# The first block's softmax sums on GpSimd's queue, with SyncE modelled in the kernel's plan

## The chip, the cores and the metric

The kernel runs on one core of a Trainium2 chip. A core has five engines that run side by side, each with its own order of instructions: TensorE (PE in the profile, with PEld for its weight loads) multiplies matrices, VectorE (DVE) and ScalarE (ACT) work element by element, GpSimd (POOL) does small work on the side, and SyncE (SP) issues DMAs. An engine that waits for a semaphore holds up everything behind it in its own order; a queue of DMAs is such an order too. The metric is the device time of one execution in microseconds (us), the median of several runs.

## What is computed

One transformer block: attention with 32 heads of 20 columns over 2048 rows, then a gated bilinear layer. The reference, cut to what matters (the feature size is 640, the gated layer's width 1728, all in bf16):

```python
qkv = (x @ wqkv).reshape(B, S, 3, H, Dh).transpose(2, 0, 3, 1, 4)
scores = einsum("bhqd,bhkd->bhqk", q, k) * (Dh ** -0.5)
o = einsum("bhqk,bhkd->bhqd", softmax(scores), v)
return o.transpose(0, 2, 1, 3).reshape(B, S, D) @ wo      # A

h  = x + A(layernorm(x), wqkv, wo)
ln = layernorm(h)
out = h + ((ln @ w_gate) * (ln @ w_up)) @ w_down
```

## The kernel before

**Tiles.** The 32 heads form eight groups of four (numbered 0 to 7), each head in a slot of 32 partitions. The queries are cut into four blocks of 512. Scores are computed transposed, keys on the partitions, into "score tiles" of 1536 columns (`sc`, two buffers in PSUM). ScalarE turns each into exponentials (`E`, line 612). VectorE can take the last 512 columns of a score tile from it and compute the exponentials there by a polynomial (lines 648 to 659); ScalarE then does only 1024. TensorE multiplies the exponentials with the values (line 836) into `acc`; a column of ones beside the values makes that product carry the sum of the exponentials too.

**Order of the work.** The first query block (b = 0) of groups 0 to 3 goes through the keys in four chunks of 512 rows, since keys and values are made on the way: chunk by chunk, rows are loaded, normalized on VectorE (`gen_ln`, with a power on GpSimd), transposed into `lnT`, and projected. The second chunk's four row tiles (t = 4 to 7) are transposed on TensorE (`on_pe`, `job_T`), the later chunks' by SP's transposing DMA (`turn`, `T_of`). Groups 4 to 7 follow over all keys at once, and their projections are made while earlier groups run. After b = 0 the other blocks follow, and each finished block's output projection and gated layer (the "tail") is worked in between the exponentials of the next.

**The plan.** One Python loop emits score tile after score tile and keeps clocks of its own (`at["pe"]`, `at["dve"]`, `at["exp"]` for ScalarE, in ns) to decide what goes in between. Three kinds of work fill the room:

- *jobs* for TensorE (projections, transposes, tails) stand in a queue and are Python generators that yield the ns of a piece; a job that yields `WAIT` is set aside in `waiting`, and `step` tries the next job, unless that one has the same key but for its kind. `ensure` forces a job whose result the next score tile needs.
- *aux* work for VectorE (normalizing, products) is stepped by `spare` when the plan's VectorE clock has room. `ensure_aux` forces it.
- *events*, registered by `later(n, fn)`, run n score tiles on.

**K and Q projections** (`job_pair`): ten matmuls into the bank `mi`, an evacuation to one of five staging tiles `st` by VectorE (line 275), then a transposing DMA on SP into `kT` or `qa`/`qb` (line 349). `read_at` tells the plan when the result can be read: 2.4 us (`MOVE_NS`) after the evacuation. Value projections (`job_vp`) need no DMA.

**Dividing by the sums** (`norm`, lines 697 to 736): each finished group's product `asb` holds four rows of sums (one per head). They are written to DRAM (line 704), read back spread over all partitions (line 705), inverted on VectorE (`back`, line 715), written to DRAM again (line 717), and read as four broadcasts (`spread`, line 722); then `times` multiplies (line 726). All seven DMAs stand on SP's queue. The second DMA of each pair is issued `TRIP` = 2 score tiles after the first. `back` comes five tiles after the copy of `asb`, and not before 6 us (`SUMS_NS`) on the plan's clock; the multiplication eight tiles after that. This is done for 42 pieces, eight of them of the first block; the rest of the groups (`FAST`) go by TensorE.

**The output weights** (`load_wo`): eight tiles, each cleared by VectorE (line 1024) and filled by four DMAs on SP (line 1031). It is an aux generator, queued behind the projections of groups 4 to 7.

## Time and profile before

| | us |
|---|---|
| median of 3 runs | 911.85 (911.7 to 914.49) |
| the profiled execution | 911.6 |
| its span, first to last instruction | 909.8 |
| ScalarE busy in it | 854.0 |
| VectorE busy in it | 752.5 |
| mean granted TensorE clock | 0.98 |

The page gives each engine's busy time and its share of the span. A view of windows gives the same by stage: engine by engine the busy us of a stretch, with the number of instructions in brackets, then the granted clock of TensorE, the share of the DMA engines in use and the GB/s moved. A row of the timeline is: start and length in us, engine, line of the kernel, operation, what it writes and reads, how many were merged (x2), and in square brackets how long the engine stood idle before it and what ended the wait. A row of the grouped view gives shapes and count, then busy us and the mean ns of one, then the idle us before. SPq is SP's queue of DMA issues: the length there is the issue, not the transfer.

### The profile page before, as it was taken

To read this page: it belongs to the slowest core of one execution; us is meant where nothing else is said; L and a number is where in the kernel's file an instruction comes from. 1 tells how busy PE (TensorE), PEld (TensorE's weight loads), DVE (VectorE), ACT (ScalarE), POOL (GpSimd) and SP (SyncE) were. 2 spreads that over 40 slices of the span, in tenths; PEclk is the share of its full clock that TensorE was granted. 3 is DMA by queue.
4 is the path that set the end of the run, shared out by engine and by line. 5 is a ranking of instruction groups with operands and counts; after the bars stand their busy time and mean duration, and the time that the engine had idled before them with its cause. 6 is when DMAs were issued, how large, how long until landed. Compare 5 with 4: busy or idle time off the path is not lost.

```text
span 909.8 us, 23209 instructions
## 1 busy us (share of the span) xinstructions
PE 814.8 (90%) x9452; PEld 408.6 (45%) x9452; DVE 752.5 (83%) x1431; ACT 854.0 (94%) x719; POOL 31.7 (3%) x163
## 2 busy tenths in 40 slices
PE   8879998979989889989988999998889989889997
PEld 6434554534223334544434445444434444435475
DVE  7678888968989989897998998998998998964242
ACT  6889999979999999999999999999999999999941
POOL 3100000000001100001000000000001000010000
PEclk9879999989999999999999999999999999999999
DMA  6342224344024455432205324302453112011310
GB/s 196 59 76 36 43 52 72 65 77 78 14 68 124 119 140 179 137 83 52 64 9 151 91 59 124 87 16 57 121 132 95 50 27 66 10 29 43 80 45 19
DMA packets 146722, 69.26 MB, mean 76 GB/s; under 512 B 73288, under 2 KB 143604, under 8 KB 146608
## 3 DMA queue, kind: packets, MB, share of 16 engines
q1 hardware_dynamic: 146608, 67.70, 30.4%
q8 instruction: 76, 1.25, 0.6%
q14 instruction: 38, 0.31, 0.1%
HBM read 48.91 MB, written 7.28 MB: 62 GB/s over the span
## 4 chain that ended last, share of the span: by engine, by line
ACT 58%; PE 19%; issue 15%; DVE 6%; DMA 2%; SPq 1%; ACTq 0%; DVEq 0%
ACT E L612 46%; ACT El L612 12%; PE sc L595 4%; PE acc L836 3%; PE mi L345 3%; PE mi L1207 2%; PE f L1189 2%; PE f L1256 1%; PE mi L545 1%; DMA xs<-in_A_x_dram 1%; DVE st L275 1%; DVE xe L653 1%; DMA sums_all<-sums 1%; PE mi L366 1%; DVE xt L659 0%
## 5 line engine op out<-in xcount | busy, mean ns | idle before, releaser
L612 ACT ACTIVATE E<-sc 128x1536 bf16<-128x1536 f32 (+1 forms) x559 | 701.7, 1403 | 14.1 <-PE sc L595 13.9
L595 PE MATMUL sc<-qa,kT 32*128 32x256 bf16 (+1 forms) x2176 | 206.2, 323 | 22.8 <-ACT E L612 15.3
L595 PEld LDWEIGHTS <-kT 32*128 32x128 bf16 x3136 | 85.8, 92 | 209.2 <-issue 168.6
L648 DVE TENSOR_SCALAR xv<-sc 128x512 f32<-128x512 f32 x198 | 136.4, 689 | 42.6 <-PE sc L595 38.4
L836 PE MATMUL acc<-E,vx 128*32 128x256 bf16 (+1 forms) x2268 | 158.5, 319 | 0.5 <-ACT E L612 0.5
L612 ACT ACTIVATE El<-sc 128x1536 bf16<-128x1536 f32 (+1 forms) x124 | 156.4, 1344 | 1.2 <-PE sc L595 1.0
L653 DVE SCALAR_TENSOR_TENSOR xe<-xt,xv 128x512 int16<-128x512 f32 x198 | 133.5, 681 | 0.7
L659 DVE SCALAR_TENSOR_TENSOR xt<-xt,xv 128x512 f32<-128x512 f32 x198 | 133.1, 680 | 0.7
L658 DVE SCALAR_TENSOR_TENSOR xt<-xv 128x512 f32<-128x512 uint16 x198 | 132.4, 682 | 0.3
L836 PEld LDWEIGHTS <-vx 128*32 128x32 bf16 x3136 | 62.3, 96 | 59.7 <-issue 57.8
L595 PE MATMUL sc<-qb,kT 32*128 32x256 bf16 (+1 forms) x960 | 68.4, 279 | 8.1 <-ACT E L612 5.1
L345 PE MATMUL mi<-wqk,lnT 128*128 128x160 bf16 x600 | 59.0, 242 | 14.7 <-DVE st L275 8.4
L1207 PE MATMUL mi<-ln2T,wu 128*128 128x256 bf16 x410 | 60.2, 277 | 7.7 <-DVE hh L1215 7.3
L1207 PE MATMUL mi<-ln2T,wg 128*128 128x256 bf16 x410 | 58.7, 274 | 8.2 <-DVE u L1212 8.2
L545 PE MATMUL mi<-kT,ident 128*128 128x512 bf16 x192 | 57.9, 383 | 5.2 <-DVE xr L1260 2.2
L345 PEld LDWEIGHTS <-lnT 128*128 128x128 bf16 x600 | 44.5, 101 | 39.4 <-issue 39.1
L1256 PE MATMUL mi<-wd,hh 128*128 128x320 bf16 x350 | 60.5, 301 | 0.9 <-DVE xr L1260 0.8
L836 PE MATMUL acc<-xe,vx 128*32 128x256 bf16 (+1 forms) x305 | 57.2, 310 | 0.0
L836 PE MATMUL acc<-El,vx 128*32 128x256 bf16 (+1 forms) x563 | 54.4, 295 | 0.0
L1256 PEld LDWEIGHTS <-hh 128*128 128x128 bf16 x448 | 38.0, 98 | 28.2 <-issue 16.6
L1207 PEld LDWEIGHTS <-wu 128*128 128x128 bf16 x410 | 35.3, 98 | 30.4 <-issue 25.4
L1207 PEld LDWEIGHTS <-wg 128*128 128x128 bf16 x410 | 35.7, 97 | 29.4 <-issue 26.0
(143 smaller groups left out, 621.6 us busy)
## 6 DMA issues: line engine op xcount, KB each, us to landing
wu<-in_B_w_up_dram SPq DMA_DIRECT2D x38, 320.0 KB
wg<-in_B_w_gate_dram SPq DMA_DIRECT2D x38, 320.0 KB
bc<-scr SPq DMA_DIRECT2D x60, 64.0 KB
bc<-scr SPq DMA_DIRECT2D x108, 32.0 KB
qsp<-qa SPq DMA_DIRECT2D x8, 384.0 KB
xr<-in_A_x_dram SPq DMA_DIRECT2D x16, 160.0 KB
out_dram<-xr SPq DMA_DIRECT2D x14, 160.0 KB
wd<-in_B_w_down_dram SPq DMA_DIRECT2D x13, 160.0 KB
```

What stands on the lines that cost most here:

```text
L345: nc.tensor.matmul(ps[:, k * PAIR:(k + 1) * PAIR], lhsT=lnT[:, c, (2 * tt + k) * P:(2 * tt + k + 1) * P], rhs=wqk[gp // 2][c][:, m, lo:lo ...
L545: nc.tensor.matmul(ps[:], lhsT=ident[:], rhs=kT[0][:, 0:2].rearrange("p t g k -> p (t g k)"), start=True, stop=True)
L595: nc.tensor.matmul(by_tile(sc[:, o:o + w]), lhsT=kT[g // 2][SLOT * j:SLOT * (j + 1), kt, g % 2, :], rhs=q_of(g, b, c0, w)[SLOT * j:SLOT * ...
L612: exps = nc.scalar.activation(e[:, 0:n_act], sc[:, 0:n_act], ACT.Exp, bias=EXP_BIAS, scale=SM_SCALE)
L648: took = nc.vector.tensor_scalar(v[:], ps, X_SCALE, X_BASE, ALU.mult, ALU.max)
L653: nc.vector.scalar_tensor_tensor(e[:], t[:], X_R, v[:], ALU.mult, ALU.add)
L658: lambda: nc.vector.scalar_tensor_tensor(t[:], u, X_P, u, ALU.add, ALU.mult),
L659: lambda: nc.vector.scalar_tensor_tensor(t[:], t[:], X_Q, u, ALU.add, ALU.mult),
L836: nc.tensor.matmul(acc["t"][SLOT * j:SLOT * (j + 1), 0:w], lhsT=vx[kt][:, VS * h:VS * h + SLOT], rhs=e, start=(acc["n"][j] == 0), stop=(ac ...
L1189: nc.tensor.matmul(ps[:, 0:n], lhsT=st["w", fp][k][:, c, f_cols(fp, f2)], rhs=st["ln2T"][:, c, c0:c0 + n], start=(c == 0), stop=(c == KT - 1))
L1207: nc.tensor.matmul(ps[:, f2 * n:(f2 + 1) * n], lhsT=st["w", fp][k][:, c, f_cols(fp, f2)], rhs=st["ln2T"][:, c, c0:c0 + n], start=(c == 0), ...
L1256: nc.tensor.matmul(ps[:, 0:HALF], lhsT=st["hh"][f // 2][:, f % 2, t * P % HW:t * P % HW + P], rhs=late["Wd"][f][:, cs], start=(f == 0), st ...
```

## The change

- In `norm`, the DMAs of the first block (b = 0) go by GpSimd's queue instead of SP's; those of the other blocks stay on SP. In both, the delay `TRIP` is gone: the read-back is issued right behind the write and waits in the queue, and so are the broadcasts behind the second write. `back` comes four tiles after the copy at the earliest (the 6 us stay), the multiplication seven after that.
- `load_wo` is queued ahead of the projections of groups 4 to 7 and works by events: every six tiles a clearing, and three tiles later its four DMAs.
- `on_pe` (the second chunk's transposes) yields `WAIT` until the plan's clock says that its rows are normalized (`rows_at`), where before it forced them at once. While such a job is set aside, `holds_up` decides which jobs may pass: those of an earlier chunk, and any that do not read these rows.
- The plan has a clock for SP (`at["sp"]`): each transpose takes 1.25 us of it (`TURN_SP`) and lands 1 us later (`TURN_END`). `read_at` follows it, a staging tile is free again only then, and `run_job` does not begin a projection before its staging tile is free. A group of output weights counts 1.7 us.

```diff
-TRIP = 2
-WO_NS, SUMS_NS, ROOT_NS, ROWS_NS = 1500, 6000, 5000, 5000
+WO_STEPS, SUMS_NS, ROOT_NS, ROWS_NS = 6, 6000, 5000, 5000
-MOVE_NS = 2400
+TURN_SP, TURN_END = 1250, 1000
...
-    staged = {"n": 0}
+    staged = {"n": 0, "free": [0] * STAGES}
...
                 if k and c == KT - 1:
+                    at["dve"] = max(at["dve"], staged["free"][n])
                     evac("dve", st[:, :, 0:DH], ps[:, 0:2 * PAIR].rearrange("p (h e) -> p h e", e=DH), 408, 68)
                     nc.sync.dma_start(dst.rearrange("p t g k -> p (t g) k"), st[:].rearrange("p h e -> p (h e)"), transpose=True)
-                    read_at[key] = at["dend"] + MOVE_NS
+                    at["sp"] = max(at["sp"], at["dend"]) + TURN_SP
+                    read_at[key] = staged["free"][n] = at["sp"] + TURN_END
...
+    def holds_up(w, key):
+        if w[0] == "T" and key[0] in ("kp", "vp", "qp"):
+            return (w[1] // TPB if len(w) == 2 else w[2] // 2) <= (key[1] if key[0] == "qp" else key[2] // 2)
+        return w[1:] == key[1:]
...
-            c = advance() if jobs and not any(w[0][1:] == jobs[0][0][1:] for w in waiting) else NEXT
+            c = advance() if jobs and not any(holds_up(w[0], jobs[0][0]) for w in waiting) else NEXT
...
-            begin = max(pe_free("F"), at["mi"], opens.get(key, 0)) + SWITCH
+            full_ = staged["free"][staged["n"] % STAGES] - 10 * 68 if key and key[0] in ("kp", "qp") else 0
+            begin = max(pe_free("F"), at["mi"], opens.get(key, 0), full_) + SWITCH
...
+        eng = nc.sync if b else nc.gpsimd
         sums = dram.tile([HPG, w], F32, name="sums", tag=f"sums{w}")
-        nc.sync.dma_start(sums[:], asb[DH:P:SLOT, 0:w])
-        later(TRIP, lambda: nc.sync.dma_start(r16, sums[:].rearrange("j (c f) -> (j c) f", f=n)))
+        eng.dma_start(sums[:], asb[DH:P:SLOT, 0:w])
+        eng.dma_start(r16, sums[:].rearrange("j (c f) -> (j c) f", f=n))
...
-            nc.sync.dma_start(scr[:].rearrange("j (c f) -> (j c) f", f=n), ri[:])
+            eng.dma_start(scr[:].rearrange("j (c f) -> (j c) f", f=n), ri[:])
             bc = nrm.tile([P, QB], F32, name="bc")
-
-            def spread():
-                for j in range(HPG):
-                    nc.sync.dma_start(bc[SLOT * j:SLOT * (j + 1), 0:w], scr[j:j + 1, :].to_broadcast([SLOT, w]))
-            later(TRIP, spread)
+            for j in range(HPG):
+                eng.dma_start(bc[SLOT * j:SLOT * (j + 1), 0:w], scr[j:j + 1, :].to_broadcast([SLOT, w]))
...
-            later(7 + TRIP - 1, mult)
-        later(4 + TRIP - 1, back)
+            later(7, mult)
+        later(4, back)
...
             done.add(("a", t))
+            rows_at[t] = at["dve"] + 780 + DVE_TAIL + DVE_PE
...
     def on_pe(t):
+        while (("a", t) not in done or at["pe"] < rows_at[t]) and not now["must"]:
+            yield WAIT
         ensure_aux(("a", t))
         yield from job_lnT(t)
...
+    def load_wo():
+        def fill_wo(g):
+            nc.vector.memset(wo[g][:], 0.0)
+            at["dve"] += 330
+            x_last[0] = None
+            later(WO_STEPS // 2, lambda: rows_wo(g))
+
+        def rows_wo(g):
+            for h in range(HPG * g, HPG * (g + 1)):
+                nc.sync.dma_start(wo[g][SLOT * (h % HPG):SLOT * (h % HPG) + DH, :], A_wo[DH * h:DH * h + DH, :])
+            at["sp"] = max(at["sp"], at["pe"]) + 1700
+        for g in range(NG):
+            later(WO_STEPS * g + 1, lambda g=g: fill_wo(g))
+
+    do(("wo",), load_wo)
     for gp in range(G1 // 2, NG // 2):
...
-    def load_wo():
-        for g in range(NG):
-            nc.vector.memset(wo[g][:], 0.0)
-            yield 230
-            due = at["pe"] + WO_NS
-            while at["pe"] < due and not now["forced"]:
-                yield WAIT
-            for j in range(HPG):
-                h = HPG * g + j
-                nc.sync.dma_start(wo[g][SLOT * j:SLOT * j + DH, :], A_wo[DH * h:DH * h + DH, :])
-
-    do(("wo",), lambda: aux.append(load_wo()))
```

More of the change, by code (lines that the diff above doesn't have):

```diff
@@ L159 @@
     now = {"i": 0, "forced": False, "must": False}
-    at = {"pe": 0, "mode": "F", "dve": 0, "dend": 0, "mi": 0, "acc": 0, "slot": [0, 0], "exp": 0, "av": {}}
+    at = {"sp": 0, "pe": 0, "mode": "F", "dve": 0, "dend": 0, "mi": 0, "acc": 0, "slot": [0, 0], "exp": 0, "av": {}}
     def x_tile(ch):
@@ L339, in job_pair @@
         ps = bank()
-        st = stages[staged["n"] % STAGES]
+        n = staged["n"] % STAGES
+        st = stages[n]
         staged["n"] += 1
@@ L953 @@
     turned = {}
+    rows_at = {}
     def turn(t):
```

## The prediction

> **What bounds the kernel now.** I read the page first, then the busy time by stage, then the waits, and last the timeline at the places where ScalarE (ACT) stood still.
>
> ```profile
> span 909.8 us, 23209 instructions
> PE 814.8 (90%) x9452; PEld 408.6 (45%) x9452; DVE 752.5 (83%) x1431; ACT 854.0 (94%) x719; POOL 31.7 (3%) x163
> ```
>
> ```profile
> core 0: us, PE busy (x) PEld busy (x) DVE busy (x) ACT busy (x) POOL busy (x), PEclk, DMA share, GB/s
> 15.00:70.00 55.00, 45.88 (x425) 22.18 (x428) 38.82 (x97) 49.38 (x38) 5.86 (x18) 0.84 0.38 74
> 70.00:140.00 70.00, 64.05 (x720) 35.14 (x712) 60.67 (x112) 70.00 (x57) 0.00 (x0) 1.00 0.27 46
> 140.00:150.00 10.00, 7.71 (x74) 4.18 (x72) 7.43 (x15) 8.27 (x8) 0.00 (x0) 0.83 0.43 84
> ...
> 195.00:210.00 15.00, 9.79 (x90) 5.04 (x88) 9.41 (x18) 9.00 (x8) 0.00 (x0) 0.77 0.40 86
> 210.00:870.00 660.00, 600.06 (x7300) 282.58 (x7298) 569.13 (x1032) 656.74 (x542) 18.59 (x43) 0.99 0.30 79
> ```
>
> The ACT column is the one to read. From 210 to 870 us it is busy for 656.74 of 660, so exponentials set the pace there and nothing in this change can take much from that stretch. What can be won lies earlier: 15 to 70 us lacks 5.6 us of ACT, 140 to 150 lacks 1.7, and 195 to 210 lacks 6.0. The views of the waits and of the timeline name the cause of the last two:
>
> ```profile
> DVE ri L715 <- DMA sums_all<-sums: 6.2, 3, 4.4
> ...
> 136.83 0.51 SPq L704 DMA_DIRECT2D sums<-qa  x1
> 138.71 0.52 SPq L705 DMA_DIRECT2D sums_all<-sums  x1
> 142.14 0.25 DVE L715 RECIPROCAL ri<-sums_all 128x16 f32<-128x16 f32 x1 [1.26 <-DMA sums_all<-sums]
> 143.66 1.02 ACT L612 ACTIVATE E<-sc 128x1024 bf16<-128x1024 f32 x1 [1.09 <-PE sc L595]
> ...
> 186.44 0.68 DVE L848 COPY asb<-acc 128x512 f32<-128x512 f32 x1
> 191.48 0.52 SPq L704 DMA_DIRECT2D sums<-asb  x1
> 194.65 1.22 SPq L349 DMA_TRANSPOSE qb<-st  x1
> 195.97 0.53 SPq L705 DMA_DIRECT2D sums_all<-sums  x1
> 197.83 0.25 DVE L715 RECIPROCAL ri<-sums_all 128x16 f32<-128x16 f32 x1 [4.43 <-DMA sums_all<-sums]
> 200.21 1.23 PE L345 MATMUL mi<-wqk,lnT 128*128 128x160 bf16 x8 [4.96 <-DVE st L275]
> 202.09 1.45 ACT L612 ACTIVATE E<-sc 128x1536 bf16<-128x1536 f32 x1 [5.02 <-PE sc L595]
> ```
>
> It is one chain twice, shown whole in the second. A reciprocal (L715) stands in VectorE's (DVE) order and waits for the softmax sums to come back from DRAM; behind it stands the evacuation that frees the projection bank; TensorE (PE) waits for that bank, and ACT for the scores behind it. At 187.1 us the sums were ready to leave (the copy of 186.44), but SP's queue, full of transposes and output-weight loads, sent them at 191.48 and read them back at 195.97. With the smaller gaps just behind it (the granted clock of these stages is down to 0.83 and 0.77), the first stall cost ACT 10 - 8.27 = 1.73 us for 1.26 of DVE's, the second 15 - 9.00 = 6.00 for 4.43: about 1.36 each. The early stage has another chain:
>
> ```profile
> 27.83 0.71 PE L288 MATMUL mi<-ident,xs 128*128 128x128 bf16 x5 [1.58 <-DVE xs L266]
> 29.19 2.79 ACT L612 ACTIVATE E<-sc 128x1536 bf16<-128x1536 f32 x2 [1.25 <-PE sc L595]
> 30.66 1.52 PE L345 MATMUL mi<-wqk,lnT 128*128 128x160 bf16 x10
> 32.83 2.79 ACT L612 ACTIVATE E<-sc 128x1536 bf16<-128x1536 f32 x2 [0.85 <-PE sc L595]
> 36.06 11.27 ACT L612 ACTIVATE E<-sc 128x1536 bf16<-128x1536 f32 x8 [0.44 <-PE sc L595]
> ...
> 38.90 0.45 PE L288 MATMUL mi<-ident,xs 128*128 128x128 bf16 x5
> ```
>
> PE has the transpose of a row tile of the second chunk in its order before VectorE has normalized it, waits 1.58 us, and the K projection that comes behind it only at 30.66 runs slowly (1.52 us for ten matmuls, in a stage whose mean clock is 0.84). The last of the four transposes runs at 38.90.
>
> **The change, part by part.** *Rows before transposes.* The planner now sets the four transposes of the second chunk aside until their rows should be there, and lets the next job pass, which is the K projection of 30.66. That should remove most of 1.25 + 0.85 + 0.44 = 2.54 us. Bounds: 0 to -2.5, and up to +5 if the rows come so late that the second chunk's scores are forced to wait (a rival below). The scores of this stage also hang on K tiles that come by SP's transposes, which do not get faster, so I take **-1.5**, under two thirds. Late next would be the transposes themselves; they are wanted for the second chunk's scores, which begin where the run of eight at 36.06 ends, at 36.06 + 11.27 = 47.3 us.
>
> *Sums by GpSimd's queue (POOL).* For the first block's eight groups, seven DMAs each leave SP for POOL: sums out, sums back, reciprocals out, four broadcasts. POOL has nothing to compute in the rows shown above from 70 to 210 us, so it can wait in line for each landing; this is why the two-step delay of the read-back can go. Nothing in this trace shows a DMA on POOL. Its price has two bounds:
>
> ```profile
> 163.38 0.51 SPq L704 DMA_DIRECT2D sums<-asb  x1
> 165.07 0.34 SPq L705 DMA_DIRECT2D sums_all<-sums  x1
> 175.36 1.91 SPq L722 DMA_DIRECT2D bc<-scr  x4
> ...
> L237 POOL TENSOR_TENSOR den<-v,half 128x4 bf16<-128x4 f32 x3 | 3.1, 1039 | 0.3
> ```
>
> Below, SP's own: 1.91/4 = 0.48 us held per DMA, and 1.7 us from issue to landing (165.07 - 163.38, the read-back having waited for it). Above, POOL's longest instruction, 1.04 us per DMA, with the landing 1.7 - 0.4 + 1.04 = 2.3 us.
>
> The lone sums of 187.1 us are served well by either: two hops end at 190.5 or 191.8, and the reciprocal stood ready at 197.83 - 4.43 = 193.4. So the 4.43 us go. I take **-5.5** of the 6.0, because the planner may put the projections there otherwise (bounds -6.0 to -4).
>
> The groups before it are crowded; groups 1, 2 and 3 had their sums ready at 121.2, 129.3 and 133.5 us (the ends of L853):
>
> ```profile
> 120.53 0.69 DVE L853 TENSOR_TENSOR qa<-acc,qa 128x512 f32<-128x512 f32 x1
> 128.60 0.68 DVE L853 TENSOR_TENSOR qa<-acc,qa 128x512 f32<-128x512 f32 x1
> 129.20 0.24 DVE L715 RECIPROCAL ri<-sums_all 128x16 f32<-128x16 f32 x1
> 132.85 0.68 DVE L853 TENSOR_TENSOR qa<-acc,qa 128x512 f32<-128x512 f32 x1
> 138.99 0.68 DVE L726 TENSOR_TENSOR on<-qa,bc 128x512 bf16<-128x512 f32 x1
> ```
>
> POOL works in order, and group 1's reciprocals (ready at 129.4) and broadcasts stand behind group 2's two hops and ahead of group 3's sums. With 0.48 us per DMA, group 2's hops are issued by 131.5, group 1's reciprocals land at 133.2 and its last broadcast at 136.3, before its multiplication, which moves one tile of some 1.2 us (660/542, from the last stretch above) ahead of 138.99, to 137.8; group 3's sums are back at 138.5, before its reciprocal, ready at 142.14 - 1.26 = 140.9. No stall, -1.7. With 1.04 us group 2's hops go out only behind group 0's broadcasts, by 134.4; the same chain lands group 1's broadcasts at 142.1 and group 3's sums at 145.5, and the stalls of groups 1 to 3 add up to some 8.8 us of DVE (4.3 + 0.3 + 1.7 + 2.5), +10.3 for ACT. The stalls begin near 0.75 us per DMA. I take 0.7, nearer SP's row, since POOL's row is that of a power computed and these DMAs compute nothing: **-1.0**.
>
> The Trainium skill (DMA: Bandwidth & Descriptors, section Latency and other measured facts) gives a first byte after about 1 us for DMAs whose descriptors GpSimd's software makes, against about 0.6 for the hardware path. By that, an estimate of 0.48 + 0.4 = 0.88 us per DMA, the same chain has 4.3 us of DVE stalls and the sum would be about 910. No run here shows it yet.
>
> *Later blocks.* They stay on SP, without the delay: SP stands 1.7 us for each landing instead of coming back two tiles later, twice in each of 34 groups. Behind it stand weight fetches and output rows. No matmul of the gated stage appears in the waits as waiting for a DMA, so there is slack to hide a few us; without that cover each would cost its 1.7. The reciprocal's earliest place moves from five tiles to four, but its due time of 6 us after the copy stays and decides at 1.2 us a tile. I take **+1.0** (bounds 0 to +3), since a stretch that is 99.5% full can hardly gain.
>
> *Output weights.* The 8 memsets and 32 fetches, of which one group's is shown at 187.15, move ahead of the projections of groups 4 to 7, whose first transposes stand at 99.22. Six tiles of 1.2 us apart, eight groups then fill some 58 us from there.
>
> ```profile
> 99.22 3.85 SPq L349 DMA_TRANSPOSE qa<-st  x2
> ...
> L1024 DVE MEMSET wo<- 128x320 uint32 x8 | 2.6, 325 | 0.1
> ...
> 187.15 1.62 SPq L1031 DMA_DIRECT2D wo<-in_A_wo_dram  x4
> ```
>
> They cost 0.325 us of DVE per group and 1.6 of SP, 12.8 us of SP in all. They are now placed among the transposes of groups 4 to 7, on a queue that the sums have left (0.51 + 0.34 + 1.91 us of SP and the reciprocals' DMA for each group). I cost the move at 0; if a transpose that a score waits for stands behind one fetch, it is 1.6 us late (bounds -0.5 to +1.6).
>
> *SP's clock in the plan.* No instruction changes. K and Q tiles get their due times from a modelled SP, 1.25 us per transpose, where the row of 194.65 shows 1.22. VectorE's takes of exponentials may shift: a whole tile costs ACT 1515 ns, one whose third VectorE takes 1096.
>
> ```profile
> L612 ACT ACTIVATE E<-sc 128x1536 bf16<-128x1536 f32 x410 | 579.9, 1515 | 11.5 <-PE sc L595 11.5
> L612 ACT ACTIVATE E<-sc 128x1024 bf16<-128x1024 f32 x149 | 157.4, 1096 | 2.6 <-PE sc L595 2.4
> ```
>
> Cost 0, bounds -2 to +4.2 (ten takes more or fewer are 4.2 us).
>
> **Sum:** -1.5 - 5.5 - 1.0 + 1.0 = -7.0 us. The profiled execution took 911.6 (span 909.8 and 1.8 around it), the runs' median is 911.85, 0.25 above, so the same sum holds for both: 911.85 - 7.0 = 904.9 us.
>
> **Rivals.** *A: POOL's queue is the new wait* (slower). Place: groups 1 to 3 of the first block, 125 to 160 us. Price: 8.8 us of DVE at 1.04 us per DMA, times 1.36 is 12 us of ACT in place of 1.7; with the other terms 911.85 + 10.3 - 5.5 - 1.5 + 1.0 = 916.2. It outweighs the gains from about 0.95 us per DMA. For it: POOL has one order, and seven DMAs with two landings in each. Against it: the sums were on a busier queue before and stalled only 1.75 us there.
>
> *B: POOL's DMAs also wait for DVE instructions*, one of 0.69 us each: 0.48 + 0.69 = 1.17 us per DMA, and by the same slope some 12.4 us of DVE, 921 us. Against it speak the rows: VectorE's work of that stretch reads scores or accumulators, or two inputs (the additions and products above). The Trainium skill (SBUF — State Buffer, the "DVE blocks DMA" trap) says that GpSimd cannot write descriptors while VectorE holds both ports; by its conditions the copies that do so read one input from SBUF and write SBUF, which these do not.
>
> *C: the rows come too late.* A wait of 5 us in the planner stands between GpSimd's root and the rows. If the second chunk's scores force them, the early gain turns into some 5 us: 904.9 + 1.5 + 5 = 911.4. Against it: the last of the transposes ran at 38.90, over 8 us ahead of that score, and what held it was PE's order.
>
> *D: the plan shifts*, ten takes fewer: 904.9 + 4.2 = 909.1.
>
> *E: it does not do what it says:* the stall of 195 us only moves, because the next projection's evacuation waits for a transpose instead. Then 911.85 - 1.5 + 1.0 = 911.4, against the trace, in which no evacuation waits for a transpose.
>
> **How the numbers follow.** Forecast 47%, A 27%, B 5%, C 8%, D 8%, E 5%. The forecast's own range is 901 to 909. For 8 in 10 I reach from 899 (all gains at their bounds) to 917, which takes in A and leaves B out. 0.3% is 2.7 us, about what a measurement of this kernel can tell from no change. Faster: 45 of the forecast and half of D, 49%. Same: 2 of the forecast, 5 of A, 5 of C, 4 of D, 5 of E, 21%. Slower: 22 of A, 5 of B, 3 of C, 30%.
>
> **What would show it.** Right: no idle time before L715 near 140 and 195 us and ACT busy 15 of 15 us there; the transposes of L288 wait for no row. A shows as idle time of DVE before L715 or L726 released by a DMA between 125 and 160 us, with POOL's issues spaced by over 0.9 us. C shows as an ACT gap at 45 to 50 us, D as another count of L648 than 198, the later blocks' cost as PE waits for weights. I am wrong if ACT's busy time in 210 to 870 us falls off by more than 3 us.

## The result and the profile after

| | before | after |
|---|---|---|
| median of 4 runs, us | 913.17 (911.7 to 914.73) | 927.79 (926.61 to 928.45) |
| ratio of the two, 95% interval | 1 | 1.0158 (1.0134 to 1.0183) |
| the profiled execution, us | 911.6 | 928.11 |
| its span, us | 909.8 | 926.3 |
| ScalarE busy, us | 854.0 | 856.2 |
| takes of VectorE (third of a score tile) | 198 | 195 |

The change makes the kernel slower by 1.6%, where 904.9 us and a gain were forecast. The first rows of the page after:

```profile
span 926.3 us, 23258 instructions
PE 827.0 (89%) x9474; PEld 411.7 (44%) x9474; DVE 745.4 (80%) x1419; ACT 856.2 (92%) x719; POOL 62.1 (7%) x219
```

ScalarE has 2.2 us more to do and 14 us more in which it does nothing. The same windows as before show where it stands (engine by engine the busy us; ACT is the fourth):

```profile
core 0: us, PE busy (x) PEld busy (x) DVE busy (x) ACT busy (x) POOL busy (x), PEclk, DMA share, GB/s
15.00:70.00 55.00, 47.44 (x489) 26.25 (x489) 38.61 (x99) 51.36 (x39) 5.88 (x18) 0.94 0.33 67
70.00:140.00 70.00, 60.19 (x625) 30.56 (x622) 57.96 (x108) 65.94 (x54) 9.32 (x17) 0.94 0.30 56
140.00:150.00 10.00, 7.34 (x72) 4.26 (x71) 4.76 (x10) 8.06 (x7) 3.66 (x7) 0.89 0.36 75
150.00:195.00 45.00, 39.49 (x404) 20.96 (x404) 34.84 (x66) 38.41 (x31) 5.67 (x11) 0.92 0.36 63
195.00:210.00 15.00, 13.55 (x150) 7.07 (x149) 13.67 (x27) 15.00 (x14) 3.69 (x7) 1.00 0.41 69
210.00:870.00 660.00, 599.84 (x7185) 279.06 (x7184) 560.69 (x1012) 647.77 (x533) 26.66 (x57) 0.98 0.30 76
```

Two of the hopes came true. The early stage lacks 55 - 51.36 = 3.6 us of ACT where it lacked 5.6, and 195 to 210 us lacks none where it lacked 6.0. But 70 to 140 us, which was full, now lacks 4.1, 150 to 195 lacks 6.6, and the long stretch from 210 to 870 us lacks 12.2 where it lacked 3.3. The view of the waits (engine, what waited, on what; us in total, times, longest) names two causes, one for each place:

```profile
PEld L1220 <- DMA wg<-in_B_w_gate_dram: 7.4, 3, 6.3
...
DVE on L732 <- DMA bc<-scr: 5.2, 2, 4.3
DVE ri L724 <- DMA sums_all<-sums: 4.9, 3, 2.8
```

**The first place, 120 to 156 us.** The timeline, GpSimd's DMAs among it:

```profile
123.20 0.68 DVE L859 TENSOR_TENSOR qa<-acc,qa 128x512 f32<-128x512 f32 x1
124.17 0.58 POOL L713 DMA_DIRECT2D sums<-qa  x1 [6.22 <-DVE ri L724]
126.26 0.68 DVE L859 TENSOR_TENSOR qa<-acc,qa 128x512 f32<-128x512 f32 x1
127.52 0.57 POOL L714 DMA_DIRECT2D sums_all<-sums  x1 [2.77 <-DMA sums<-qa]
128.08 0.55 POOL L726 DMA_DIRECT2D scr<-ri  x1
130.20 2.00 POOL L729 DMA_DIRECT2D bc<-scr  x4 [1.57 <-DMA scr<-ri]
132.19 0.58 POOL L713 DMA_DIRECT2D sums<-qa  x1
134.88 0.57 POOL L714 DMA_DIRECT2D sums_all<-sums  x1 [2.10 <-DMA sums<-qa]
...
136.90 0.25 DVE L724 RECIPROCAL ri<-sums_all 128x16 f32<-128x16 f32 x1 [2.81 <-DMA sums_all<-sums]
137.41 1.99 POOL L729 DMA_DIRECT2D bc<-scr  x4 [1.42 <-DMA scr<-ri]
138.83 1.45 ACT L620 ACTIVATE E<-sc 128x1536 bf16<-128x1536 f32 x1 [2.17 <-PE sc L603]
139.38 0.58 POOL L713 DMA_DIRECT2D sums<-qa  x1
143.79 0.57 POOL L714 DMA_DIRECT2D sums_all<-sums  x1 [3.82 <-DMA sums<-qa]
145.66 0.25 DVE L724 RECIPROCAL ri<-sums_all 128x16 f32<-128x16 f32 x1 [1.05 <-DMA sums_all<-sums]
146.57 1.99 POOL L729 DMA_DIRECT2D bc<-scr  x4 [1.67 <-DVE on L732]
151.18 0.69 DVE L732 TENSOR_TENSOR on<-qa,bc 128x512 bf16<-128x512 f32 x1 [4.25 <-DMA bc<-scr]
155.07 1.02 ACT L620 ACTIVATE E<-sc 128x1024 bf16<-128x1024 f32 x1 [5.35 <-PE sc L603]
```

Groups 1 and 2 have their sums ready at 123.9 and 126.9 us, 3.1 apart; before, it was 121.2 and 129.3, 8.1 apart. So group 2's sums are ready before POOL has sent group 0's broadcasts. They leave at 132.19, 5.3 us late, and the reciprocal of 136.90 waits 2.81 us. The rest follows like beads: group 3's sums leave 5.3 us late too, its reciprocal waits 1.05, a multiplication 4.25. That is 8.1 us of VectorE, and ScalarE's gaps behind them. How much of it is POOL's doing is seen below, where x4 keeps the plan's edits and leaves the sums on SP.

**The second place, one example.** SP's queue, then TensorE and ScalarE, in the first stretch of a later block's tail:

```profile
373.24 0.64 SPq L726 DMA_DIRECT2D scr<-ri  x1
377.58 2.85 SPq L729 DMA_DIRECT2D bc<-scr  x4
380.48 0.42 SPq L1061 DMA_DIRECT2D qsp<-qa  x1
...
381.47 0.44 SPq L1168 DMA_DIRECT2D wg<-in_B_w_gate_dram  x1
...
386.35 0.34 PEld L1220 LDWEIGHTS <-wg 128*128 128x128 bf16 x3 [6.26 <-DMA wg<-in_B_w_gate_dram]
387.83 1.45 ACT L620 ACTIVATE E<-sc 128x1536 bf16<-128x1536 f32 x1 [5.72 <-PE sc L603]
```

SP sends the reciprocals at 373.24 and stands until 377.58 for their landing, since the broadcasts, now next in line, read them. The gate weights behind go out at 381.47. The gated matmul stands in TensorE's order and waits 6.26 us for them, and ScalarE 5.72 us for the scores behind. With the two gaps right after it (0.70 and 0.80 us) this place makes 7.2 of the 13.0 us of gaps behind 215 us; none of the others is longer than 1.0.

### The profile page after: what moved, and what is told of

It is laid out like the page before. It is cut to its first block, busy times and chain, and to the rows that moved or that the text cites. A ratio compares the mean times of both kernels' runs of the same rounds, so it can differ in the third digit from the quotient of the medians.

```text
span 926.3 us, 23258 instructions
## 1 busy us (share of the span) xinstructions
PE 827.0 (89%) x9474; PEld 411.7 (44%) x9474; DVE 745.4 (80%) x1419; ACT 856.2 (92%) x719; POOL 62.1 (7%) x219
## 3 DMA queue, kind: packets, MB, share of 16 engines
q8 instruction: 76, 1.25, 0.6%
## 4 chain that ended last, share of the span: by engine, by line
ACT 54%; PE 19%; issue 15%; DVE 7%; DMA 4%; POOL 1%; SPq 0%; ACTq 0%; DVEq 0%; POOLq 0%
ACT E L620 43%; ACT El L620 11%; PE sc L603 4%; PE acc L842 3%; PE mi L1220 2%; PE f L1202 2%; PE mi L345 1%; PE mi L368 1%; PE mi L552 1%; PE f L1269 1%; PE mi L1269 1%; DMA kT<-st 1%; DVE xv L656 1%; DMA scr<-ri 1%; DVE xe L661 1%
## 5 line engine op out<-in xcount | busy, mean ns | idle before, releaser
L656 DVE TENSOR_SCALAR xv<-sc 128x512 f32<-128x512 f32 x195 | 134.1, 688 | 46.5 <-PE sc L603 43.3
L620 ACT ACTIVATE El<-sc 128x1536 bf16<-128x1536 f32 (+1 forms) x124 | 163.8, 1404 | 1.4 <-PE sc L603 1.4
L842 PE MATMUL acc<-E,vx 128*32 128x256 bf16 (+1 forms) x2245 | 161.1, 321 | 0.7 <-DVE qa L859 0.5
L667 DVE SCALAR_TENSOR_TENSOR xt<-xt,xv 128x512 f32<-128x512 f32 x195 | 130.4, 680 | 0.4
L666 DVE SCALAR_TENSOR_TENSOR xt<-xv 128x512 f32<-128x512 uint16 x195 | 129.7, 681 | 0.4
L552 PE MATMUL mi<-kT,ident 128*128 128x512 bf16 x214 | 65.6, 388 | 4.6 <-DVE hh L1228 1.4
L842 PE MATMUL acc<-xe,vx 128*32 128x256 bf16 (+1 forms) x302 | 61.3, 312 | 0.0
L842 PE MATMUL acc<-El,vx 128*32 128x256 bf16 (+1 forms) x589 | 60.1, 296 | 0.0
L1228 DVE TENSOR_TENSOR hh<-mi,u 128x512 bf16<-128x512 f32 x49 | 33.7, 687 | 21.0 <-PE mi L1220 20.2
```

What stands on the lines that cost most here:

```text
L552: nc.tensor.matmul(ps[:], lhsT=ident[:], rhs=kT[0][:, 0:2].rearrange("p t g k -> p (t g k)"), start=True, stop=True)
L620: exps = nc.scalar.activation(e[:, 0:n_act], sc[:, 0:n_act], ACT.Exp, bias=EXP_BIAS, scale=SM_SCALE)
L656: took = nc.vector.tensor_scalar(v[:], ps, X_SCALE, X_BASE, ALU.mult, ALU.max)
L666: lambda: nc.vector.scalar_tensor_tensor(t[:], u, X_P, u, ALU.add, ALU.mult),
L667: lambda: nc.vector.scalar_tensor_tensor(t[:], t[:], X_Q, u, ALU.add, ALU.mult),
L842: nc.tensor.matmul(acc["t"][SLOT * j:SLOT * (j + 1), 0:w], lhsT=vx[kt][:, VS * h:VS * h + SLOT], rhs=e, start=(acc["n"][j] == 0), stop=(ac ...
```

## The experiments

All ratios are against the kernel before, timed on the same chip beside the kernel (its medians there were 911.2 to 911.7 us, and 913.17 for the change). The gaps are ScalarE's in each profiled execution: its idle time before every exponential but the first, added up by stage, in us. The last column gives how far apart in time the sums of groups 0, 1, 2 and 3 of the first block are ready.

| kernel | median us | ratio (95%) | gaps 15-70 | 70-170 | 170-215 | 215-end | groups 0 to 3 ready, us apart |
|---|---|---|---|---|---|---|---|
| before | | 1 | 5.0 | 1.7 | 6.0 | 1.9 | 5.3, 8.1, 4.3 |
| after | 927.79 | 1.0158 (1.0134 to 1.0183) | 3.0 | 12.6 | 0 | 13.0 | 9.0, 3.1, 7.2 |
| x1 | 912.49 | 1.0007 (0.9981 to 1.0033) | 4.9 | 1.4 | 7.5 | 1.9 | |
| x2 | 905.76 | 0.9938 (0.991 to 0.9966) | 4.3 | 2.5 | 0 | 0.2 | 5.3, 8.1, 4.3 |
| x4 | 907.82 | 0.9960 (0.9928 to 0.9992) | 0.6 | 7.5 | 0 | 3.1 | 9.0, 3.1, 7.2 |
| x5 | 910.49 | 0.9988 (0.9963 to 1.0013) | 1.2 | 1.4 | 10.3 | 1.4 | 7.0, 6.4, 8.1 |
| x6 | 904.35 | 0.9900 (0.9863 to 0.9937) | 6.2 | 3.3 | 0 | 4.6 | 7.0, 3.9, 10.6 |
| x7 | 911.48 | 0.9985 (0.9964 to 1.0006) | 4.7 | 0.1 | 5.6 | 6.2 | 7.4, 3.9, 9.3 |
| x9 | 911.63 | 0.9989 (0.9965 to 1.0012) | 1.2 | 12.1 | 0 | 0.4 | 9.0, 3.1, 7.2 |
| x10 | 908.88 | 0.9956 (0.993 to 0.9982) | 1.7 | 6.8 | 0 | 5.1 | |
| x3 | 916.44 | 1.0041 (1.0019 to 1.0064) | 0.4 | 10.8 | 0 | 8.5 | |
| x8 | 924.13 | 1.0140 (1.0103 to 1.0177) | 0.6 | 8.4 | 0 | 11.4 | |
| y1 | 915.62 | 1.0050 (1.0019 to 1.0081) | 0.5 | 12.6 | 0 | 5.0 | |
| y3 | 916.35 | 1.0040 (1.0016 to 1.0063) | 1.5 | 10.7 | 0 | 4.4 | |
| y5 | 921.49 | 1.0097 (1.0065 to 1.013) | 0.5 | 12.1 | 0 | 8.8 | |
| x11 | 908.10 | 0.9943 (0.9906 to 0.998) | 0.5 | 5.7 | 3.7 | 1.8 | 7.0, 6.4, 8.0 |
| x12 | 908.18 | 0.9951 (0.9918 to 0.9984) | 3.6 | 5.4 | 0 | 0.4 | 7.0, 3.9, 13.6 |
| x14 | 906.40 | 0.9924 (0.9886 to 0.9963) | 3.3 | 0.7 | 0 | 5.5 | 7.0, 3.9, 10.6 |

The gaps belong to one execution each, and some of these stand at the edge of their kernel's runs: x8's took 917.73 us, its fastest of five, y3's and y5's are the fastest of theirs too, x6's took 910.06, its slowest of five, and x3's 918.10, its slowest of nine. So the profiles of x3 and x8 are 0.4 us apart where the medians are 7.7, and the step between these two is read from the medians, not from the sums of the gaps. From before to after the gaps grow by 14.0 us, and three takes fewer cost ScalarE 3 x 0.42 = 1.3; together 15.3 of the 16.5 us of span.

### The two halves of the sums' edit in the old order, and the change without one half

x1: the kernel before, the later blocks' DMAs at once on SP, nothing else in another place.

```diff
-        later(TRIP, lambda: nc.sync.dma_start(r16, ...))
+        read_back = lambda: nc.sync.dma_start(r16, ...)
+        if b:
+            read_back()
+        else:
+            later(TRIP, read_back)
...
-            later(TRIP, spread)
+            if b:
+                spread()
+            else:
+                later(TRIP, spread)
```

> The kernel before, with one edit: in the blocks after the first, SP reads the sums back and spreads the reciprocals right behind the write, without the delay of two score tiles. The order on TensorE, VectorE and ScalarE is exactly that of before. Theory 1 (SP stands in line for each landing, and the weight fetches behind it come late): slower by 4 to 10 us, with TensorE waiting for wu or wg loads between 210 and 870 us and ScalarE idle there well above the 3.3 us of before. Rival (the changed kernel's loss in the later blocks, some 9 us of ScalarE, comes from its other order of work, not from the wait itself): within 2.7 us of before.

x2: the kernel before, the first block's seven DMAs per group on POOL and at once; the order of PE, DVE and ACT as before.

```diff
-        nc.sync.dma_start(sums[:], asb[DH:P:SLOT, 0:w])
+        eng = nc.sync if b else nc.gpsimd
+        at_once = not b
+        eng.dma_start(sums[:], asb[DH:P:SLOT, 0:w])
...
-            later(TRIP, spread)
+            if at_once:
+                spread()
+            else:
+                later(TRIP, spread)
```

> The kernel before, with one edit: the first block's seven DMAs per group go by GpSimd's queue, each right behind the one before it. All other orders are exactly those of before, the multiplication a tile later than in the changed kernel. Theory 2 (GpSimd's queue is in order, and groups 1 to 3 crowd on it): the 5 us gap near 200 us is gone (-6), while VectorE waits 2 to 6 us for sums or broadcasts between 125 and 155 us (+1 to +6 of ScalarE above the 1.7 of before), together -4 to +1 us. Rival (the queue is quick enough, and the stalls of the changed kernel come from its earlier multiplications and other spacing): no such wait, -6 to -7.7 us.

x3: the kernel after, its later blocks with the delay and the places of before.

```diff
+        if b:
+            later(2, read_back)
+        else:
+            read_back()
...
+            if b:
+                later(2, spread)
+            else:
+                spread()
...
-            later(7, mult)
-        later(4, back)
+            later(8 if b else 7, mult)
+        later(5 if b else 4, back)
```

> The changed kernel, with the delay of two score tiles given back to the blocks after the first (and with it the fifth and eighth tile). Theory 1: it regains most of the 9 us that the changed kernel loses between 210 and 870 us, 917 to 922 us, and no matmul of the gated stage waits several us for weights. Rival: the loss there is the plan's, and the time stays at 924 to 929 us.

x4: the kernel after with all of `norm` as before, which leaves the three edits of the plan (rows, output weights, SP's clock).

```diff
-        eng = nc.sync if b else nc.gpsimd
-        eng.dma_start(sums[:], asb[DH:P:SLOT, 0:w])
+        nc.sync.dma_start(sums[:], asb[DH:P:SLOT, 0:w])
...
-        later(4, back)
+        later(4 + TRIP - 1, back)
```

> The changed kernel with the sums' whole round trip as before (SP, both delays, all blocks): what is left is the waiting transposes, the early output weights and SP's clock in the plan. Theory (these three are worth the 2 us that ScalarE gains before 70 us, and the output weights out of the way shorten the stall near 200 us): 904 to 911 us. Rival (the new plan itself spoils the later order): 914 to 920 us.

Measured, as the ratio's distance from 1 times 912 us: x1 +0.6 (no change that can be told, as its rival had it), x2 -5.7 (the rival's gain, though with some of the theory's waits), x4 -3.6 (within its theory's range); as a sum -8.7, near what the prediction gave, while the whole change is +14.4. None of these three edits costs anything in company of the kernel before. A fourth part, the reciprocals and multiplications a tile earlier, was not run alone there. x2 shows what POOL's queue costs in the order of before; VectorE's waits are these:

```profile
DVE ri L721 <- DMA sums_all<-sums: 0.9, 1, 0.9
DVE on L735 <- DMA bc<-scr: 0.9, 1, 0.9
```

The same seven DMAs on the same queue go with 1.7 us of VectorE's waiting here, where the groups come 5.3, 8.1 and 4.3 us apart, and with 8.1 us in the change, where they come 9.0, 3.1 and 7.2 apart. x3 came out at 916.44 us, just under its theory's range, with no wait over 0.8 us for weights. It shows that the later blocks' half, delay and places together, is worth 1.0158 - 1.0041 = 0.0117, 11 us, in the new order, though by x1 to take the delay away costs nothing in the old one.

### Which edit of the plan does what

x5: only the rows' wait; x6: only the output weights; x7: only SP's clock.

```diff
+            c = advance() if jobs and not any(holds_up(w[0], jobs[0][0]) for w in waiting) else NEXT
...
+        while (("a", t) not in done or at["pe"] < rows_at[t]) and not now["must"]:
+            yield WAIT
...
```

> The kernel before with the waiting transposes alone (rows_at and holds_up). Theory 3 (this alone removes the early gaps; it starts the next stages some 4 us earlier and leaves the rest): ScalarE's idle time from 15 to 70 us falls from 5.0 to under 1.5 us, the stall near 200 us stays, 906 to 909 us. Rival (the earlier chunks crowd the four groups' sums between 115 and 150 us, as in the run with all three plan edits, where that stretch idled 7.5 us against 1.7): idle time of 70 to 170 us over 4 us, 909 to 913 us.

```diff
-    do(("wo",), lambda: aux.append(load_wo()))
+    do(("wo",), load_wo)
     for gp in range(G1 // 2, NG // 2):
...
```

> The kernel before with the output weights' clearing and fetching moved ahead, alone. Theory 3: the stall near 200 us goes (SP's queue is free there; -6 us), and the stretch from 70 to 170 us does not change by more than 1 us: 905 to 907 us. Rival (the fetches on SP at 100 to 160 us hold up the first four groups' sums and make the 7.5 us of idle time seen there with all three edits): -6 us and +4 to +6 us, 909 to 913 us.

```diff
-                    read_at[key] = at["dend"] + MOVE_NS
+                    at["sp"] = max(at["sp"], at["dend"]) + TURN_SP
+                    read_at[key] = staged["free"][n] = at["sp"] + TURN_END
...
```

> The kernel before with SP's clock in the plan, alone. Theory 3: little moves, within 2.7 us of before, all three known stalls still there. Rival (the clock spaces the projections otherwise and so moves the groups' sums together): idle time of 70 to 170 us over 4 us, slower by 2 to 5 us.

x5 takes 3.8 us from the early gaps, 2.3 of it from the three gaps of 29 to 36 us that the prediction weighed, and gives 4.3 back at the stall of 195 us, which grows from 6.0 to 10.3; so it stays at 910.49 us, where its theory had 906 to 909. x6 has the lowest ratio of the single edits, though its interval overlaps x2's: with the fetches gone from SP's queue at 187 us the stall of 195 is 0, without POOL. In their new place they go with 1.6 us more of gaps at 70 to 170 us, where its theory allowed 1. x7 changes nothing that can be told. All three change how far apart the first groups come, though none touches those groups. Why the plan moves them so, edit by edit, was not traced.

### From x4 to the change, one step at a time

x9: x4 with the first block's DMAs on POOL as in x2. x10: x4 with only the two DMAs of the sums on POOL. Both keep x4's order.

```diff
-        nc.sync.dma_start(sums[:], asb[DH:P:SLOT, 0:w])
+        eng = nc.sync if b else nc.gpsimd
+        eng.dma_start(sums[:], asb[DH:P:SLOT, 0:w])
...
```

> The kernel with the three plan edits and the old sums (907.8 us, 7.5 us of idle time from 70 to 170 us), with the first block's seven DMAs per group put on GpSimd's queue at once, the tile counts kept: TensorE, VectorE and ScalarE have exactly its order. Theory 2 (with this plan the groups' sums come closer together, and GpSimd's one order holds group 2's and 3's sums behind broadcasts): idle time from 70 to 170 us 8 us or more, 908 to 914 us, so GpSimd's queue costs here what it gained in the plan of before. Rival (what hurts in the changed kernel is the multiplication a tile earlier): under 4 us there, 901 to 905 us.

> The same, with only the two hops of the sums on GpSimd's queue; the reciprocals and the broadcasts stay on SP with their delay. Same order on the other engines. Theory 2: the sums no longer stand behind broadcasts, VectorE's waits before the reciprocal go to under 1 us, idle time from 70 to 170 us under 5 us and 902 to 907 us. Rival (the landing itself is slow there, whoever is in front): VectorE still waits 3 us before a reciprocal, 908 us or more.

x8: the change with only the places of the later blocks' reciprocals and multiplications as before, so it has x3's order and differs in the delay of the later DMAs alone.

```diff
-            later(7, mult)
-        later(4, back)
+            later(8 if b else 7, mult)
+        later(5 if b else 4, back)
```

> The changed kernel with five and eight tiles in the later blocks as before, but still without the delay of their DMAs: TensorE, VectorE and ScalarE have exactly the order of the run that had the delays back (916.4 us), only SP's queue differs. Theory 1 (the wait in SP's line holds up the gated stage's weights, in this order of work as it did not in the order of before): 922 to 929 us, with waits for wg or wu. Rival (the changed kernel's 11 us came from the earlier tiles, so from the plan): 914 to 919 us.

The chain in ratios: before 1, x4 0.9960, x9 0.9989 (POOL's queue), x3 1.0041 (first block one tile earlier), x8 1.0140 (later DMAs at once), after 1.0158 (later blocks one tile earlier). In x2 POOL's queue gains 5.7 us, in x9 it gains nothing against x4 (the intervals overlap): x4 has no stall at 195 us left to remove, and the gaps of 70 to 170 us grow from 7.5 to 12.1. VectorE's waits for DMAs in that stretch, x4's and then x9's:

```profile
DVE ri L724 <- DMA sums_all<-sums: 4.0, 2, 3.5
DVE on L735 <- DMA bc<-scr: 0.9, 1, 0.9
```

```profile
DVE on L744 <- DMA bc<-scr: 4.0, 1, 4.0
DVE ri L730 <- DMA sums_all<-sums: 3.4, 2, 2.9
```

So with the plan's three edits VectorE waits 4.9 us here though the sums are on SP, and 7.4 us with them on POOL. Of the change's 12.6 us of gaps in this stretch, 7.5 come with the plan's edits whatever the queue, and POOL's queue adds some 4.6.

The biggest step is x3 to x8, +0.0099 or 9 us with the instructions of PE, DVE and ACT in one order; the last one is within its intervals. The step x9 to x3, 4.7 us, is just clear of them (1.0012 and 1.0019). Its gaps do not grow at 70 to 170 us (12.1 to 10.8) but behind 215 us (0.4 to 8.5): there a reciprocal of the first block, which comes a tile earlier than x9's, waits 3.31 us at 229.1 for sums on POOL, and ScalarE 2.4 us behind it. The rest of this step was not traced. x10's theory failed: no reciprocal waits over 0.2 us there, but a multiplication waits 3.5 us for broadcasts on SP, the gaps are x4's, and it took 908.88 us where 902 to 907 were expected. Its interval overlaps x9's.

### What the later blocks' step costs it for

y1: x8 with the queries' copies (`qsp`, line 1061) fifty tiles later. y3: x8 with only the broadcasts two tiles later, the read-back still at once. y5: x8 with the later blocks' DMAs on POOL too.

```diff
-RES_STEPS, WD_AT, WD_STEPS, SPILL_AT = 3, 10, 2, 60
+RES_STEPS, WD_AT, WD_STEPS, SPILL_AT = 3, 10, 2, 110
```

> The changed kernel with the old tile counts in the later blocks (924.1 us), the 16 copies of the queries to DRAM (qsp) 50 score tiles later; same order on TensorE, VectorE and ScalarE. Theory 1a (the copies' traffic stretches the landings that SP waits for, and the weights behind them come late): the wait of 4 to 6 us for wg near 376 us is gone, 915 to 920 us. Rival 1b (the wait itself is enough, whatever the traffic): 922 to 926 us, the wait for wg still over 3 us.

```diff
-            for j in range(HPG):
-                eng.dma_start(bc[SLOT * j:SLOT * (j + 1), 0:w], scr[j:j + 1, :].to_broadcast([SLOT, w]))
...
+            if b:
+                later(2, spread)
+            else:
+                spread()
```

> The same kernel (924.1 us) with only the broadcasts of the later blocks delayed again by two tiles, the read-back at once; same order. If SP's wait for the reciprocals' landing ahead of the broadcasts is what holds up wg (the longest such wait was 3.6 us): 915 to 919 us, as with both delays. If the wait for the sums' landing does it (the longest 4.1 us): 921 to 925 us.

```diff
-        eng = nc.sync if b else nc.gpsimd
+        eng = nc.gpsimd
```

> The same kernel (924.1 us) with the later blocks' DMAs on GpSimd's queue too, at once; same order on TensorE, VectorE and ScalarE. Theory 1 (it is SP's line that holds up the weights): no matmul waits over 1 us for wg or wu, 912 to 918 us. Rival (the landing traffic, whoever waits for it, delays the weights): still a wait of 3 us or more near 376 us, 921 us or more.

SP's rows at the same place in x8, and then in x3:

```profile
364.49 0.60 SPq L726 DMA_DIRECT2D scr<-ri  x1
368.86 2.70 SPq L729 DMA_DIRECT2D bc<-scr  x4
...
372.61 0.46 SPq L1168 DMA_DIRECT2D wg<-in_B_w_gate_dram  x1
```

```profile
370.99 0.64 SPq L730 DMA_DIRECT2D scr<-ri  x1
...
372.94 0.58 SPq L1178 DMA_DIRECT2D wg<-in_B_w_gate_dram  x1
375.92 2.62 SPq L735 DMA_DIRECT2D bc<-scr  x4
```

From reciprocals to gate weights it takes 8.1 us in x8 and 1.95 in x3, where the weights go out ahead of the broadcasts. The waits for the weights, x8's, y1's and y5's:

```profile
PEld L1220 <- DMA wg<-in_B_w_gate_dram: 5.9, 2, 4.9
```

```profile
PEld L1220 <- DMA wg<-in_B_w_gate_dram: 1.1, 2, 0.8
```

```profile
DVE ri L724 <- DMA sums_all<-sums: 12.3, 8, 3.4
...
PEld L1220 <- DMA wg<-in_B_w_gate_dram: 0.6, 2, 0.4
```

y3 takes all of the step back (1.0040 beside x3's 1.0041): what hurts is the broadcasts' wait in line, not the read-back's. y1 takes it back too (1.0050), with the copies gone from beside the reciprocals and no wait for weights over 0.8 us. Two of its rows, SP's queue again:

```profile
369.62 0.34 SPq L726 DMA_DIRECT2D scr<-ri  x1
371.09 1.72 SPq L729 DMA_DIRECT2D bc<-scr  x4
```

Without copies the broadcasts follow 1.5 us behind the reciprocals, beside them 4.3 or 4.4. So the loss needs both: SP standing for a landing, and the traffic just ahead of it. In x8 a pair of copies and two weight fetches go out within 2.3 us ahead of the reciprocals; in y1 there are no copies, and the last fetch is 3.6 us ahead, so how much of the longer landing is the copies' own is not shown. y5 frees SP, and no matmul waits over 0.4 us for weights, as its theory had it. But VectorE then waits 12.3 us in eight places for sums on POOL, it took 921.49 us where 912 to 918 were expected, and its interval overlaps x8's: no cure.

### Parts put together in the old plan

x11: x2 and the rows' wait. x12: x2 and the output weights. x14: the output weights and only the two DMAs of the sums on POOL, with the reciprocals and broadcasts on SP with their delay.

```diff
+        eng = nc.sync if b else nc.gpsimd
+        eng.dma_start(sums[:], asb[DH:P:SLOT, 0:w])
+        if b:
+            later(TRIP, read_back)
+        else:
+            read_back()
...
+    do(("wo",), load_wo)
...
```

> The plan of before with two edits: the first block's DMAs on GpSimd's queue (905.8 us alone) and the waiting transposes (910.5 alone, its 10 us gap near 200 us being the one that GpSimd's queue takes away). If gains add up where no stall is shared: early idle time near 1.2 us, none near 200 us, 900 to 903 us. Rival (the earlier start crowds the groups on GpSimd's queue): idle time from 70 to 170 us over 6 us, 906 to 910 us.

> The plan of before with two edits: the first block's DMAs on GpSimd's queue and the output weights early (904.4 us alone). Both take away the same stall near 200 us, so theory: 903 to 906 us, no sum of the two gains. Rival (the early weights crowd the first groups on GpSimd's queue): idle time from 70 to 170 us over 6 us, 908 to 912 us.

> The plan of before with two edits: only the two hops of the first block's sums on GpSimd's queue (reciprocals and broadcasts on SP with the delay), and the output weights early. Theory 2 (the sums of group 3 stand behind broadcasts when all seven DMAs share GpSimd's order; with five of them off it they do not): idle time from 70 to 170 us under 2.5 us, none near 200 us, 900 to 904 us. Rival (the early weights on SP hold up the broadcasts in turn): 4 us or more of idle time there, 905 to 909 us.

x11 and x12 are no better than x2, though x5 and x6 move the gaps that x2 leaves: with the rows' wait a gap of 3.7 us comes back at 170 to 215 us, and with the output weights groups 1 and 2 come 3.9 us apart and a reciprocal waits 3.2 us for sums on POOL. None of x11, x12 and x14 came as low as its theory (900 to 903, 903 to 906, 900 to 904 us).

x2, x9, x11 and x12 each have the order of a kernel whose sums are on SP: before, x4, x5 and x6. Against these, POOL's queue adds 0.8, 4.6, 4.3 and 2.1 us to the gaps of 70 to 170 us. The distance between the groups alone does not set this, for x11's are 7.0, 6.4 and 8.0 us apart. In x11 group 3's sums are ready at 133.4 us and leave at 138.25, since group 2's reciprocals (133.59) and broadcasts (136.28) stand ahead of them in POOL's order; the reciprocal behind waits 3.1 us. In x5 SP sends the same sums at 134.75.

x14 takes four broadcasts and the reciprocals' DMA per group from POOL's order, and its windows are nearly full:

```profile
70.00:170.00 100.00, 91.63 (x1006) 49.10 (x1004) 88.58 (x168) 99.34 (x82) 5.95 (x10) 1.00 0.30 57
170.00:215.00 45.00, 40.85 (x444) 21.64 (x445) 40.12 (x73) 45.00 (x38) 2.28 (x4) 1.00 0.47 80
```

Yet 5.5 us of gaps turn up behind 215 us, and its interval overlaps x12's and x2's. x6 (0.9900), x14 (0.9924) and x2 (0.9938) all beat both kernels; which is best, their intervals leave open.

## Why the prediction was wrong

The step that failed is the one called **Sum**: four terms, each priced in the order of work of before, added up. The three parts measured alone (x1, x2, x4) add to -8.7 us, near the -7.0 forecast; the change makes +14.4. Two things were missed. Two parts may remove one and the same stall, so the gain counts once; and the plan's edits, priced at 0 or at their own stall alone, change when the sums and the weights are wanted, by which the next part's price changes: POOL's queue from -5.7 us (x2) to nothing that can be told (x4 to x9), the later blocks' DMAs at once from +0.6 (x1) to +9 (x3 to x8). By its points:

- *Rows before transposes, -1.5.* The mechanism was right and its local gain larger (3.8 us in x5, 2.0 in the change), but in x5 the kernel gained nothing from it that can be told (0.9988): the stall of 195 us took it back.
- *Lone sums, -5.5.* Right with the old plan (the gap of 6.0 is 0 in x2), but not owed to POOL alone: the output weights' move does it as well. In the change the term was already spent.
- *Output weights, 0 (bounds -0.5 to +1.6).* Wrong: x6 is -9 us. The prediction quoted the fetch of 187.15 in the very queue that sent the sums late, and priced only what the fetch does in its new place, not what it leaves behind.
- *Crowded groups, -1.0, and rival A.* Wrong even in the order in which it was priced: in x2 VectorE waits 1.7 us, and the gaps of 70 to 170 us grow by 0.8 where they were to shrink by 1.0. POOL's issue was taken as 0.7 us per DMA and came out cheaper; these are the change's rows:

```profile
L729 POOL DMA_DIRECT2D bc<-scr x32 | 15.9, 503 | 13.4 <-DMA scr<-ri 8.8 <-DVE on L732 4.7
L714 POOL DMA_DIRECT2D sums_all<-sums x8 | 4.6, 574 | 16.8 <-DMA sums<-qa 10.1 <-DMA sums<-asb 6.7
L726 POOL DMA_DIRECT2D scr<-ri x8 | 4.4, 548 | 18.9 <-DVE ri L724 18.9
L713 POOL DMA_DIRECT2D sums<-qa x4 | 2.6, 638 | 61.9 <-DVE qa L859 55.6 <-DVE ri L724 6.2
```

  The mean of one is 0.50 to 0.64 us, and by the prediction's own threshold of 0.75 no stall should have come. What was too small is the landing: 1.7 to 2.3 us in the sum, while in x2 the reader of a group's sums or reciprocals goes out 2.0 to 3.7 us behind their write. Rival A came at its place without its condition, 0.95 us per DMA, and that it came near its size (8.1 us of VectorE for 8.8, 12.6 us of gaps for 12) is luck: 7.5 of the 12.6 are in x4, with the sums on SP. What decides is what stands ahead in POOL's order when a group's sums are ready, and the prediction took that order from before as fixed.
- *Later blocks, +1.0 (bounds 0 to +3).* Right in the old order (x1: +0.6), wrong by three times its upper bound in the new one (x3 to x8: 9 us). The landing was priced at 1.7 us, where it is 4.3 at the place shown, and the cover ("slack to hide a few us") ended there. The view of before's waits was not quite empty either: one weight load of the gated stage waits 0.2 us for `wg`.
- *SP's clock, 0.* In its bounds (0.9985).
- *Rival B* was not seen: POOL's broadcasts took 503 ns with VectorE 80% busy. *C* was not seen: the early gaps shrank. *D* is three takes, 1.3 us. *E* is refuted, the stall of 195 us is gone and not moved.
- The sign named for being wrong came: ACT's busy time of 210 to 870 us fell from 656.74 to 647.77, by 9 us where 3 were the limit.

The Trainium skill (DMA: Bandwidth & Descriptors, section Latency and other measured facts) gives GpSimd's DMAs a later first byte than SP's, by some 0.4 us. The landing agrees roughly: group 1's sums and their read-back go out 2.04 us apart on POOL in x2 (122.59 and 124.63), and 1.72 us apart on SP in before (121.78 and 123.50). The 0.88 us per DMA that the prediction worked out from it, as a time that POOL is held, does not, with 0.50 to 0.64 measured.

Not settled: the step from x8 to after (its intervals overlap), most of the 4.7 us from x9 to x3, and which of the plan's decisions turns 8.1 us between groups into 3.1.

## What to carry to other kernels

A gain worked out from a stall is owed to that stall, not to the edit: before adding two gains, ask whether both remove the same wait, and whether the edit of a plan's times leaves the order in which the other was priced. A wait for a landing may stand in a shared queue of DMAs only where nothing that is needed soon is queued behind; there, its price is not the landing but the landing under the traffic of that moment plus all that stands in line. Where several edits are made together, run each alone and the whole less each: here every part that was run alone looked harmless.

## What was not expected of the hardware

The same DMA, four rows of reciprocals to DRAM, had its reader start 1.5 us behind its issue in quiet (y1) and 4.3 us (373.24 to 377.58, in the change) right behind a pair of query copies and two weight fetches; its issue too took 0.64 us in place of 0.34. And POOL holds its queue little longer per DMA than SP (0.50 to 0.64 us in the mean of each kind, beside 0.42 to 0.55 for the first block's on SP in before); what it lost in line were its waits for landings, up to 3.82 us between the two hops of one group's sums.
